# A long convolution fused with an MLP on one core: one chunk of batch 1's first stage ahead of the MLP instead of a chunk and a half

## The chip, the cores and the metric

The kernel runs on one core of a Trainium2 chip. The metric is the device time of one execution in microseconds. The engines are TensorE (PE), VectorE (DVE), ScalarE (ACT), GpSimd (POOL) and SyncE (SP, which here only issues DMAs).

## The reference

```python
def _attn_ref(x, v, pos_emb, w1, w2):            # x, v: (2, 12480, 128)
    h_mlp = np.maximum(pos_emb @ w1, 0.0) @ w2
    h_filt = h_mlp * np.exp(-0.01 * pos)[:, None]
    u = x * v
    y = irfft(rfft(u, 2 * S) * rfft(h_filt, 2 * S))[:, :S]    # along the sequence
    return x * y
def _moe_ref(x, w_in, w_out):                    # x: (24960, 128), w_in: (128, 2048)
    h = x @ w_in
    return np.maximum(0.01 * h, h) @ w_out
```

The output of the first function, both batches behind each other, is the input of the second. All is float32.

## The kernel before, in words

The convolution is a transform in two stages of matmuls each way, over a grid of 98 x 128 points. Per batch there are: stage 1 (98-point transforms of u = x * v, in chunks of 4 columns, 16 chunks), stage 2 (128-point transforms, the product with the filter's spectrum, and the transform back, in 25 chunks of 4 rows), and the last transform, tile by tile (32 tiles of 390 tokens per batch), whose result is multiplied by x, turned, and fed to the MLP. The numbers between the stages go through DRAM (`scr1`, `scr1b`, `scr2`).

Batch 0's stage 1 and 2 run first, alone. Then the MLP's loop over token blocks k and 128-wide parts f of the hidden layer starts (`m1`, `m2`; one pair (k, f) is a step i = 16 k + f of three plus three matmuls). Between its steps, the loop does batch 1's stages 1 and 2 in small pieces: the generator `conv1` (lines 418 to 463), which a `next(conv)` moves on by a piece. Half a chunk of stage 1 is four `next`: at the second of them come 8 matmuls (line 438) and a copy by ScalarE (line 98), then an addition and a subtraction by VectorE (lines 100, 102). "A piece" in this document is such a half chunk. `pace(i)` (line 1207) says how many `next` must be done by step i: none more before step 14, and all of stage 1 by step 120. `AHEAD` is how many were done before the loop.

A chunk of batch 1's stage 1 needs three things first: `fetch_a(c)` (line 240: seven DMAs on SyncE's queue, ft from the table cf, line 243, and x and v, lines 67 and 69), `mult_a(c)` (line 254: GpSimd's product x * v, line 256), and the place of its result `o1`, whose store to `scr1b` (line 460) comes a chunk later. In the steady state of `conv1`, the fetch of chunk c + 1 is issued as chunk c begins, and its product is issued behind chunk c's first half; both hold only from chunk `PRE` on. The chunks below it are fetched and multiplied by other code: chunks 0 and 1 in the loop of batch 0's stage 2 (lines 817 to 820) and behind it (line 863), and chunk `PRE` itself by the MLP's step 2 (`fetch_a(PRE)`, line 1158) and step 9 (`mult_a(PRE)`, lines 1151 and 1160).

Batch 0's stage 2 (lines 807 to 866) works a chunk i as follows: the filter's part (`hp`, line 830, copied by ScalarE, stored as hspec by DMAs of ScalarE's queue, line 840), the forward transform `up` (line 129), six products on VectorE (GpSimd takes one of them, but not in the last two chunks; lines 137 and 138), the transform back of the chunk before (`dp`, line 157), its copies (lines 232 and 795) and stores. Between them, `weights()` (lines 701 to 755) turns the MLP's weights from float64 into pairs of float32 parts. Behind the last chunk stands the handover: the last rows go straight from SBUF into tile 0's input (`last_c`, line 650), tile 1's and 2's inputs are loaded (`upper_c`, `load_gx`, `rows_c`), two pieces of `conv1` are made while tile 0's rows are on their way (lines 1188 to 1194, their VectorE part being put off to lines 1199 and 1155), and tile 0 is transformed (`front0`).

The tiles' inputs pass GpSimd as well (`join_hi`, `join_lo`, lines 668, 677, 680), and so does the second part of the MLP's input (zl, line 950). Each engine works its instructions in the order in which the code issues them.

Of the kernel before, what the change touches and what calls it, by code (L numbers as in the profile page):

```python
# [30 lines left out]
def tile_conv_mlp(ctx, tc, x, v, pos_emb, w1, w2, w_in, w_out, cf, cr, cg, cb, ci, cw, out):  # L31
# [6 lines left out]
    NCH = (NA + KC - 1) // KC  # L38
# [82 lines left out]
    def chunk(c):  # L121
        k0 = c * KC
        return k0, min(KC, NA - k0)
# [112 lines left out]
    with tc.manual_schedule():  # L236
# [3 lines left out]
        def fetch_a(c):  # L240
            ft = s0.tile([128, MC1 * 4 * NA], F32, tag="s0", name="ft1", bufs=3)[:NA].rearrange(
                "a (m p e) -> a m p e", m=MC1, p=2)
            nc.sync.dma_start(out=ft, in_=cf[:, c * MC1:(c + 1) * MC1])
            xv = []
            for i, src in enumerate((x, v)):
                t = s0.tile([128, 1024], F32, tag=f"s{1 + i}", name="xv1", bufs=3 - i)[:NA, :2 * MC1 * D].rearrange(
                    "a (p m d) -> a p m d", p=2, d=D)
                load_tokens(t, src[1], c * MC1, MC1)
                xv.append(t)
            got[c] = ft, xv  # L250
# [3 lines left out]
        def mult_a(c):  # L254
            ft, (xt, vt) = got.pop(c)
            nc.gpsimd.tensor_tensor(out=xt, in0=xt, in1=vt, op=ALU.mult)
            u1[c] = ft, xt
# [155 lines left out]
        psc = {}  # L413
        N1 = HB // MC1
        WAIT = 12
        PRE = 2

        def conv1():
            late = None
            for c in range(N1):  # L420
                if PRE <= c < N1 - 1 and c + 1 not in got:
                    fetch_a(c + 1)
# [7 lines left out]
                for h in range(MC1 // 2):  # L430
# [22 lines left out]
                    yield  # L453
                    if h == 0 and PRE <= c < N1 - 1:
                        mult_a(c + 1)
# [109 lines left out]
        conv = conv1()  # L565
        pieces = N1 * (MC1 // 2) * 4 + WAIT + 3 + 15 * NCH - 3
        A0 = 0
        AHEAD = 1 + 4 * (A0 + 3)

        mlp = ctx.enter_context(tc.tile_pool(name="mlp", bufs=2, reuse_waits="tile"))  # L570
        class Ring:
# [118 lines left out]
        with ExitStack() as st:  # L690
# [66 lines left out]
            load_b(ORD[0])  # L757
            load_b(ORD[1])
            wprep = weights()
            FETCH = [NCH - 5, NCH - 2]  # L760
            late = []
            turn = [0]

# [8 lines left out]
            def ahead(n):  # L772
                for _ in range(4 * n):
                    next(conv)
# [32 lines left out]
            for i, c in enumerate(ORD):  # L807
                if i + 2 < NCH:
                    load_b(ORD[i + 2])
                if NCH - 10 <= i < NCH - 5:  # L810
                    next(first_c)
                if i == NCH - 2:
                    load_gx(0)
                if i == NCH - 1:
                    load_gx(1)
                    rows_c(0, 0, 0, (MID - 2) * KC)
                if i in FETCH:
                    fetch_a(FETCH.index(i))
                if i == NCH - 2:
                    mult_a(0)  # L820
                for f in late:
                    f()
                late = []
                n = chunk(c)[1]
                t, es = bins.pop(c), eh.pop(c)
                hp = two("h")
                for ri in range(2):
                    for k in range(n):
                        h, j = 64 * (k % 2), ri * n // 2 + k // 2
                        nc.tensor.matmul(hp[k % 2][:, D * j:D * j + D], es[h:h + 64, k // 2, ri, :], w22[h:h + 64, :],  # L830
                                         start=True, stop=True)
                hs = sbb.tile([128, 2, KC // 2, 2, D], F32, tag="hs", name="hs", bufs=2)
                for k in range(2):
                    nc.scalar.copy(hs[:, :, :n // 2, k, :],
                                   hp[k][:, :n * D].rearrange("p (r j d) -> p r j d", r=2, d=D))
                hs = hs.rearrange("p r j i d -> p r (j i d)")
                up = two("u")
                fwd(up, lambda s: t[:, :n, s, FO:], n)
                for s in range(2):
                    nc.scalar.dma_start(out=hspec[c][:, :, s, :n * D], in_=hs[HB * s:HB * s + HB, :, :n * D])  # L840
                if i + 1 < NCH:
                    hidden(ORD[i + 1])
                for _ in range(3):
                    next(wprep, None)
                pins[c] = sbb.tile([128, 2, 512], F32, tag="pin", name="pin", bufs=2)
                ab = [sbb.tile([128, 2, 512], F32, tag=g, name=g) for g in ("ta", "tb")]
                product(ab, up, hs, n * D, pins[c], nc.vector if i >= NCH - 2 else nc.gpsimd)
                if i >= 1:
                    b4 = ORD[i - 1]
                    dps[b4] = two("d")  # L850
                    back_halves(dps[b4], pins.pop(b4), b4)
                    evac(b4)
                for _ in range(2):
                    next(wprep, None)
# [3 lines left out]
                    f()  # L858
                late.clear()

            ahead(1)
            run(wprep)
            mult_a(1)
            dps[ORD[-1]] = two("d")
            back_halves(dps[ORD[-1]], pins.pop(ORD[-1]), ORD[-1])
            evac(ORD[-1])
# [283 lines left out]
        at(2, "piece", 0)  # L1150
        at(9, "mult", PRE)

        def do(what, t, i):
            if what == "piece":
                run(pieces_out.pop(0))
                for f in psc.pop("held"):
                    f()
                fetch_a(PRE)
            elif what == "mult":
# [24 lines left out]
        SLOTS = ends[NT] - 14  # L1184
        done = AHEAD
        pieces_out = []
# [27 lines left out]
        for k in range(NTL):  # L1214
            for f in range(NF):
                i = k * NF + f
# [84 lines left out]
```

## Time and profile before

| | |
|---|---|
| median of the runs shown | 1609.13 us |
| lowest run | 1602.2 us |
| the profiled execution's own time | 1607.94 us |
| its span, from the first to the last instruction | 1606.1 us |
| TensorE busy | 1552.2 us, 97% of the span |
| VectorE, ScalarE, GpSimd busy | 71%, 62%, 48% |
| mean granted TensorE clock | 0.985 |

The profile is of one execution. "Busy" leaves out instructions that only issue a DMA or wait. "PEld" is TensorE's loading of weights, beside the matmuls; a float32 matmul of this code counts as two records. The chain of waits goes back from the last instruction to whatever released each one, so a stretch of it that lists only TensorE was bound by TensorE. In a timeline, the square bracket gives how long the engine was idle before the instruction and what released it. "SPq" and "ACTq" are the DMA-issuing instructions of SyncE and ScalarE, and their time is that of the issue, not of the transfer.

### The profile page before, as it was taken

How to read it: one execution, taken by the hardware profiler on the slowest of the kernel's cores; microseconds unless marked ns; L12 is line 12 of the kernel's file. 1: busy time of each engine (PE TensorE's matmuls, PEld its weight loads, DVE VectorE, ACT ScalarE, POOL GpSimd, SP SyncE). 2: the span in 40 equal slices, each digit the busy share in tenths (PEclk: the TensorE clock that was granted, in tenths of full speed). 3: DMA queues.
4: the chain of work that ended last, by engine and by line, in shares of the span. 5: the costliest groups of instructions: out<-in, count | busy, mean ns of one | idle time of the engine just before them, and what ended most of it. 6: DMA issues, size and time to landing. Idle time of an engine off the chain costs nothing.

```text
span 1606.1 us, 27353 instructions
## 1 busy us (share of the span) xinstructions
PE 1552.2 (97%) x9173; PEld 1318.8 (82%) x9173; DVE 1137.9 (71%) x1785; ACT 997.1 (62%) x2108; POOL 766.7 (48%) x806
## 2 busy tenths in 40 slices
PE   7995999899999999999999999999999999999998
PEld 7884555588888888888888888988888888888888
DVE  6884888656985565666676775677777777777776
ACT  2331544446655476777776766667777676777776
POOL 6772212145754275867777774543443433334310
PEclk9997999999999999999999999999999999999999
DMA  9997999866767466756656661421212212121200
GB/s 273 305 314 250 318 317 335 256 196 189 227 199 220 132 190 185 206 158 182 173 167 180 172 163 37 130 86 58 73 54 64 79 58 90 52 64 61 64 11 21
DMA packets 166268, 253.30 MB, mean 158 GB/s; under 512 B 14240, under 2 KB 118932, under 8 KB 163056
## 3 DMA queue, kind: packets, MB, share of 16 engines
q1 hardware_dynamic: 146388, 226.28, 47.4%
q10 hardware_dynamic: 19740, 25.28, 4.6%
q8 instruction: 73, 1.20, 0.3%
q14 instruction: 67, 0.55, 0.1%
HBM read 168.03 MB, written 83.43 MB: 157 GB/s over the span
## 4 chain that ended last, share of the span: by engine, by line
PE 75%; DMA 12%; DVE 7%; ACT 2%; issue 2%; SPq 1%; POOL 0%; ACTq 0%; DVEq 0%; POOLq 0%
PE mh L993 28%; PE acc L1035 9%; PE acc L1034 9%; PE acc L1036 9%; PE yp L917 4%; PE cv L143 3%; DMA scr<-o 3%; PE cv L438 3%; DMA scr<-ct 3%; PE op L1066 2%; PE a L392 2%; PE up L129 2%; PE zp L936 1%; DMA ft<-in_cf_dram 1%; PE dp L157 1%
## 5 line engine op out<-in xcount | busy, mean ns | idle before, releaser
L998 DVE SCALAR_TENSOR_TENSOR rl<-mh,rh 128x512 fp32r<-128x512 f32 (+1 forms) x336 | 226.9, 682 | 203.2 <-ACT rh L997 201.8
L1006 DVE TENSOR_TENSOR rl<-mh,rh 128x512 fp32r<-128x512 f32 (+2 forms) x416 | 277.1, 670 | 83.7 <-ACT rh L1005 75.1
L1001 ACT ACTIVATE mh<-mh 128x512 f32<-128x512 f32 (+2 forms) x416 | 236.4, 569 | 154.1 <-PE mh L993 141.1
L993 PE MATMUL mh<-zh,w_in_h 128*128 128x512 f32 (+3 forms) x800 | 316.8, 396 | 3.4 <-DVE rl L998 2.3
L993 PE MATMUL mh<-zl,w_in_h 128*128 128x512 f32 (+3 forms) x800 | 300.1, 375 | 0.0
L993 PE MATMUL mh<-zh,w_in_l 128*128 128x512 f32 (+3 forms) x800 | 299.9, 375 | 0.0
L1035 PE MATMUL acc<-rl,w_out_h 128*128 128x512 f32 (+3 forms) x800 | 299.3, 374 | 0.1
L1034 PE MATMUL acc<-rh,w_out_h 128*128 128x512 f32 (+3 forms) x800 | 299.3, 374 | 0.0
L1036 PE MATMUL acc<-rh,w_out_l 128*128 128x512 f32 (+3 forms) x800 | 299.0, 374 | 0.0
L997 ACT ACTIVATE rh<-mh 128x512 fp32r<-128x512 f32 (+1 forms) x336 | 198.9, 595 | 138.8 <-PE mh L993 130.1
L950 POOL TENSOR_TENSOR zl<-zf,zh 128x390 fp32r<-128x390 f32 (+24 forms) x110 | 68.4, 634 | 402.4 <-ACT zh L949 386.1
L680 POOL TENSOR_TENSOR cp<-cq,cp 98x256 f32<-98x256 f32 x248 | 193.3, 780 | 31.4 <-DVE cp L668 14.7
L1003 DVE CAST rh<-mh 128x512 fp32r<-128x512 f32 (+2 forms) x208 | 139.3, 670 | 65.9 <-ACT mh L1001 65.6
L993 PEld LDWEIGHTS mh<-zh,w_in_h 128*128 128x128 f32 x800 | 151.9, 190 | 29.4 <-DVE rl L998 8.4
L993 PEld LDWEIGHTS mh<-zh,w_in_l 128*128 128x128 f32 x800 | 151.9, 190 | 19.8
L1035 PEld LDWEIGHTS acc<-rl,w_out_h 128*128 128x128 f32 x800 | 151.3, 189 | 20.3 <-DVE rl L1006 0.4
L1034 PEld LDWEIGHTS acc<-rh,w_out_h 128*128 128x128 f32 x800 | 151.3, 189 | 19.8
L1036 PEld LDWEIGHTS acc<-rh,w_out_l 128*128 128x128 f32 x800 | 151.3, 189 | 19.8
L993 PEld LDWEIGHTS mh<-zl,w_in_h 128*128 128x128 f32 x800 | 152.3, 190 | 15.2 <-DVE zl L982 0.2
L1005 ACT CAST rh<-mh 128x512 fp32r<-128x512 f32 (+2 forms) x208 | 118.5, 570 | 6.5
L677 POOL TENSOR_TENSOR cq<-cin 98x256 f32<-98x256 f32 x124 | 97.1, 783 | 0.5 <-DMA cin<-scr 0.4
L138 POOL TENSOR_TENSOR pin<-ta,tb 128x512 f32<-128x512 f32 (+1 forms) x23 | 28.8, 1252 | 134.9 <-DVE tb L137 134.9
(166 smaller groups left out, 2545.7 us busy)
## 6 DMA issues: line engine op xcount, KB each, us to landing
cin<-scr SPq DMA_DIRECT2D x318, 98.0 KB
hd<-hspec SPq DMA_DIRECT2D x48, 512.0 KB
bin<-scr SPq DMA_DIRECT2D x24, 768.0 KB
scr<-o SPq DMA_DIRECT2D x28, 588.0 KB
scr<-ct SPq DMA_DIRECT2D x25, 512.0 KB
scr1b<-o SPq DMA_DIRECT2D x32, 392.0 KB
hspec<-hs ACTq DMA_DIRECT2D x48, 256.0 KB
xm<-in_x_dram SPq DMA_DIRECT2D x128, 96.0 KB
```

Source lines behind the costliest of these rows:

```text
L677: eng.tensor_tensor(out=cq[:, p], in0=ci_t[:, 0, :, 0, :], in1=ci_t[:, 0, :, 1, :], op=op)
L680: eng.tensor_tensor(out=cp[:, p, w], in0=cq[:, p], in1=cp[:, p, 1], op=op)
L993: nc.tensor.matmul(hp, u[:, fs], m, start=(i == 0), stop=(i == 2))
L997: nc.scalar.activation(out=split2(rh), in_=plain(hp), func=AF.Relu)
L998: nc.vector.scalar_tensor_tensor(out=split2(rl), in0=plain(hp), scalar=0.0, in1=split2(rh), op0=ALU.max, op1=ALU.subtract)
L1001: nc.scalar.activation(out=hp, in_=hp, func=AF.Lrelu, alpha=0.01)
L1003: nc.vector.tensor_copy(split2(rh), plain(hp))
L1005: nc.scalar.copy(split2(rh), plain(hp))
L1006: nc.vector.tensor_tensor(out=split2(rl), in0=plain(hp), in1=split2(rh), op=ALU.subtract)
L1034: nc.tensor.matmul(ap, w_out_h[:, f, :], rh, start=(f == 0 and not sums(k)), stop=False)
L1035: nc.tensor.matmul(ap, w_out_h[:, f, :], rl, start=False, stop=False)
L1036: nc.tensor.matmul(ap, w_out_l[:, f, :], rh, start=False, stop=(f == NF - 1))
```

## The change

Of chunks 0 and 1, only chunk 0 is fetched and multiplied in batch 0's stage 2, and no piece is made there: the call `ahead(1)`, `mult_a(1)` and the second fetch go. `PRE` is 1 instead of 2, so chunk 1 is the one that step 2 fetches and step 9 multiplies, and `conv1` fetches chunk 2 itself, as it begins chunk 1. `AHEAD` is 9 instead of 13, so that `pace` spreads four `next` more over the steps 14 to 120.

```diff
-        PRE = 2
+        PRE = 1
...
-        AHEAD = 1 + 4 * (A0 + 3)
+        AHEAD = 1 + 4 * (A0 + 2)
...
-            FETCH = [NCH - 5, NCH - 2]
...
-                if i in FETCH:
-                    fetch_a(FETCH.index(i))
+                if i == NCH - 5:
+                    fetch_a(0)
                 if i == NCH - 2:
                     mult_a(0)
...
-            ahead(1)
             run(wprep)
-            mult_a(1)
             dps[ORD[-1]] = two("d")
```

Chunk 1 begins, in `conv1`, at the end of the second piece of the handover, where the loads of tile 2 have not been issued yet. So chunk 2 is fetched there, ahead of chunk 1. On SyncE's queue the handover reads as follows in the kernel before, from the last load of tile 1 (`cin`, line 643) over tile 2's loads to the store of chunk 0 and the fetch of chunk 2:

```order
L643 DMA cin<-scr_0_63 49x512 x2
L622 DMA cin<-scr_0_63 49x512 x3
L626 DMA cin<-scr_0_63 49x2x128 x2
L643 DMA cin<-scr_0_63 49x512 x2
L602 DMA gt<-in_cg_dram 49x392 x2
L608 DMA xm<-in_x_dram 48x2x256 x2
L610 DMA xm<-in_x_dram 1x2x256
L613 DMA xm<-in_x_dram 1x256
L460 DMA scr1b<-o_1265 98x4x256 x2
L243 DMA ft_3126<-in_cf_dram 98x1568
```

and in the changed kernel, from the same load of tile 1 on:

```order
L643 DMA cin<-scr_0_63 49x512 x2
L243 DMA ft_3017<-in_cf_dram 98x1568
L67 DMA xv_3019<-in_x_dram 96x2x512
L67 DMA xv_3019<-in_x_dram 1x2x512
L69 DMA xv_3019<-in_x_dram 1x2x512
L67 DMA xv_3023<-in_v_dram 96x2x512
L67 DMA xv_3023<-in_v_dram 1x2x512
L69 DMA xv_3023<-in_v_dram 1x2x512
L622 DMA cin<-scr_0_63 49x512 x3
L626 DMA cin<-scr_0_63 49x2x128 x2
L643 DMA cin<-scr_0_63 49x512 x2
L602 DMA gt<-in_cg_dram 49x392 x2
```

A whole fetch, chunk 2's, has come in between tile 1's and tile 2's loads; the fetch of chunk 1 follows where that of chunk 2 stood, behind the store of line 460.

On TensorE, the end of batch 0's stage 2 and the handover up to tile 0's transform (`yp`, `zp`) read, in the kernel before (the number in a name tells the tiles of chunk 0, xv_2618, from those of chunk 1, xv_2834):

```order
L129 MATMUL up<-bin,mb 64x512 x4
L746 MATMUL wcp<-wo,wts 128x128 x2
L157 MATMUL dp<-pin,mi_69 128x512 x4
L438 MATMUL hp<-xv_2618,ft_2616 98x128 x8
L157 MATMUL dp<-pin,mi_69 128x512 x4
L438 MATMUL cv<-xv_2618,ft_2616 98x128 x8
L438 MATMUL cv<-xv_2834,ft_2832 98x128 x8
L965 MATMUL yp<-cp,gt 64x128 x8
```

and in the changed kernel, whose lines behind the change are three lower (L962 is L965 before):

```order
L129 MATMUL up<-bin,mb 64x512 x4
L746 MATMUL wcp<-wo,wts 128x128 x2
L157 MATMUL dp<-pin,mi_69 128x512 x8
L438 MATMUL cv<-xv_2618,ft_2616 98x128 x16
L962 MATMUL yp<-cp,gt 64x128 x8
```

The piece between the two groups of L157 is gone, and the two pieces of the handover are both chunk 0's.

## Rows read from the trace of the kernel before

**Rows 1.** The page's first line.

```profile
span 1606.1 us, 27353 instructions
```

**Rows 2.** Windows: stretch, length, busy us (records) by engine, PEclk, DMA share, GB/s.

```profile
340.00:360.00 20.00, 20.00 (x134) 18.64 (x133) 9.57 (x17) 10.79 (x25) 10.78 (x14) 1.00 0.62 177
...
420.00:440.00 20.00, 19.78 (x140) 17.46 (x139) 18.76 (x22) 11.39 (x23) 15.56 (x13) 1.00 0.71 220
...
480.00:600.00 120.00, 119.31 (x721) 105.36 (x720) 73.13 (x115) 67.45 (x138) 53.33 (x57) 1.00 0.63 180
```

**Rows 3.** Chain of waits, 290 to 320 us: start, length, what.

```profile
291.65 4.71 DMA gt<-in_cg_dram
...
296.39 0.52 ACTq L840
...
308.43 0.64 PE wcp L746 x4
...
310.99 1.92 PE hp L438 x16
312.91 3.01 PE dp L157 x8
...
315.94 0.70 DVE ct L795
```

**Rows 4.** Timeline of the same end of stage 2, all engines.

```profile
284.68 0.43 DVE L740 TENSOR_TENSOR w_out_l<-wo,w_out_h 128x256 fp32r<-128x256 f32 x1 [3.31 <-ACT w_out_h L738]
...
297.58 1.16 PE L830 MATMUL hp<-w,es 64*128 64x128 f32 x16 [2.18 <-ACT es L786]
...
307.18 2.36 POOL L256 TENSOR_TENSOR xv<-xv,xv 98x1024 f32<-98x1024 f32 x1 [7.46 <-DMA xv<-in_v_dram]
...
307.83 1.99 DVE L740 TENSOR_TENSOR w_out_l<-wo,w_out_h 128x256 fp32r<-128x256 f32 x1 [1.08 <-ACT w_out_h L738]
...
313.17 0.69 DVE L138 TENSOR_TENSOR pin<-ta,tb 128x512 f32<-128x512 f32 x1
...
313.92 0.30 PEld L157 LDWEIGHTS dp<-pin,mi 64*128 64x128 f32 x4 [0.79 <-DVE pin L138]
```

**Rows 5.** Timeline, TensorE, the handover's pieces and tile 0's transform.

```profile
315.84 3.74 PE L438 MATMUL cv<-xv,ft 98*98 98x128 f32 x32
...
320.92 1.07 PE L965 MATMUL yp<-cp,gt 98*64 98x128 f32 x8 [1.34 <-issue]
```

**Rows 6.** Chain of waits: one piece in the loop.

```profile
347.95 1.75 PE cv L438 x16
```

**Rows 7.** Timeline, SyncE's DMA issues of a store and of two fetches.

```profile
329.81 0.84 SPq L460 DMA_DIRECT2D scr1b<-o  x2
...
335.85 0.57 SPq L69 DMA_DIRECT2D xv<-in_v_dram  x1
...
352.83 0.33 SPq L243 DMA_DIRECT2D ft<-in_cf_dram  x1
...
356.46 0.57 SPq L69 DMA_DIRECT2D xv<-in_v_dram  x1
```

**Rows 8.** Timeline, GpSimd, products of two chunks and what follows.

```profile
342.55 2.36 POOL L256 TENSOR_TENSOR xv<-xv,xv 98x1024 f32<-98x1024 f32 x1
346.91 0.41 POOL L950 TENSOR_TENSOR zl<-zf,zh 128x122 fp32r<-128x122 f32 x1 [2.00 <-ACT zh L949]
...
360.97 2.37 POOL L256 TENSOR_TENSOR xv<-xv,xv 98x1024 f32<-98x1024 f32 x1 [7.44 <-DMA xv<-in_v_dram]
```

**Rows 9.** Windows behind the handover's pieces.

```profile
320.00:322.00 2.00, 1.06 (x8) 0.61 (x8) 1.90 (x5) 0.20 (x1) 0.00 (x0) 1.00 0.71 196
322.00:324.00 2.00, 1.08 (x9) 0.75 (x10) 0.83 (x3) 0.00 (x0) 0.00 (x0) 0.76 0.46 169
```

**Rows 10.** Waits of GpSimd, 340 to 560 us: total, times, longest.

```profile
POOL xv L256 <- DMA xv<-in_v_dram: 36.3, 7, 11.5
```

**Rows 11.** Group of the pieces' matmuls, 326 to 600 us: busy, mean, idle before.

```profile
L438 PE MATMUL cv<-xv,ft 98*98 98x128 f32 x464 | 56.3, 273 | 0.7 <-DVE o L102 0.7
```

## The prediction

> **What bounds the kernel now.** I read the page's head first: one execution spans 1606.1 us [rows 1] and was timed at 1607.94 us, so 1.84 us lie around the span. Then the busy time by stretch: from 340 us on TensorE is busy 20.00 of 20 us, and still 119.31 of 120 us from 480 to 600 us [rows 2]. So in the MLP every matmul added costs its own time, and work on other engines costs nothing until one of them fills up: VectorE has 18.76 of 20 us between 420 and 440 us, while TensorE still has 19.78 [rows 2].
>
> The place of the change is the handover from batch 0's second stage to the MLP, 290 to 350 us. There I read the chain of waits [rows 3]. From 297.58 us [rows 4] to 315.92 us the chain is TensorE alone, and the piece of batch 1's convolution that the change takes away stands in it with 1.92 us (L438 at 310.99), directly ahead of the last chunk's inverse matmuls (L157, 3.01 us). Behind them come the copy on VectorE at 315.94, three small DMA issues, and the DMA that hands the last rows to tile 0. A chain only says what came last, so I asked the timeline what the L157 matmuls would have waited for without the piece [rows 4]. Their weight load at 313.92 waited 0.79 us for VectorE's product (L138, 313.17 to 313.86). So VectorE, not the piece, sets the end of this stage; the piece sat in TensorE's gap.
>
> VectorE itself was held there. L740 took 1.99 us where the same instruction took 0.43 us at 284.68, and it ended at 309.82, 0.28 us behind GpSimd's product of chunk 1 (L256, 307.18 to 309.54) [rows 4]. GpSimd started that late because it waited 7.46 us for chunk 1's v rows. The change removes that product from this place.
>
> **The change, part by part.** The instruction totals of the built program do not change on any engine; all terms are moves.
>
> (a) Stage end, removed: chunk 1's fetch (seven DMAs; by the shapes 98 x 1568 floats of cf and twice 98 x 1024 of x and v, 1.42 MB), GpSimd's product, and a first piece (8 matmuls, one ScalarE copy, two VectorE operations). Without the GpSimd product L740 ends at 307.83 + 0.43 = 308.26. The next VectorE instruction then waits for the wcp matmul, which ends at 308.43 + 0.64 = 309.07 [rows 3]. So the VectorE series that ran without a gap from 309.82 to 313.86 starts at about 309.1: **0.7 us earlier**. TensorE follows it, since the piece is gone. Bounds: 0 if another wait holds VectorE; 1.92 us, the chain's price of the piece, if TensorE's order alone had mattered. I take 0.7, the nearest rows. The piece's ScalarE copy and VectorE operations came after the product, in idle time, and are worth nothing. The freed DMA bandwidth is worth nothing on a chain that is TensorE from 297.58 on.
>
> (b) The handover keeps two pieces (now chunk 0's halves instead of chunk 0's second and chunk 1's first): 3.74 us from 315.84, in the wait for tile 0's rows. The first transform starts at 320.92 after an idle time of 1.34 us [rows 5], so they stay covered, in either version.
>
> (c) The MLP gets one piece more: 1.75 us of TensorE by the chain at 347.95 [rows 6], **+1.75 us**. TensorE has no idle time to take it. Its VectorE part, two operations on 512 columns like L138 with its 0.69 us [rows 4], is hidden wherever VectorE is not full; by the stretch 420 to 440 it might not be, which would add up to 1.4 us. From below: 0, if the piece falls where TensorE waits anyway. I take 1.75.
>
> (d) Moved on SyncE: chunk 2's fetch (seven issues) now stands ahead of tile 2's loads, and chunk 1's fetch takes chunk 2's old place behind the store of chunk 0. A fetch issued without hindrance takes 352.83 to 357.03, 4.2 us [rows 7]. So tile 2's loads start that much later, and so does the fetch behind them. Its last issue, at 335.85, becomes 340.05. The chunk that was fetched at 352.83 had its last issue at 356.46, and GpSimd, waiting for it, began at 360.97 [rows 7, 8]: 4.5 us from issue to use. So chunk 1 is there at 344.55; GpSimd, which in the old order took its chunk at 342.55 without a wait [rows 8], multiplies 344.6 to 346.9. The first piece in the MLP stood at 347.95 and would stand 0.7 us earlier at most: no stall, with a margin of 0.3 to 1 us. Two microseconds of GpSimd's waiting are covered by the 2.00 us it idled behind the old product [rows 8]. Cost 0; from above see the second rival.
>
> Sum: 1607.94 - 0.7 + 1.75 = **1609.0 us**. The median shown is 1609.13, the lowest run 1602.2; the profiled execution lies 1.2 us under that median, so the sum stands at the median too. It is no change that could be told: about 2% (32 us) is what a measurement of this kernel can tell.
>
> **Weighed against a page.** In the two stretches from 320 to 324 us TensorE was busy 1.06 and 1.08 of 2 us, and its granted clock, 1.00 in the first, was 0.76 on the mean of the second: it fell there from its upper level, 2.4 GHz, to its lower, 1.2 GHz [rows 9]. What the engine did before the fall was to work in two short bursts, waiting for VectorE between them; (a) leaves a like gap ahead of L157's last matmuls, where the piece stood. The Trainium skill ("TensorE: Matmul & The Clock Gate", Part 1, "What's actually happening") has the clock follow how busy the engine was shortly before, which speaks against this change. If the new gap lowers the clock, the third rival's time follows; the sum leaves it out, because the gap is one where those two stretches had several.
>
> **Rivals.**
>
> *The stage end gains more.* ScalarE's issue of hspec at 296.39 had to wait for the landing of gt (291.65 + 4.71), and TensorE idled 2.18 us behind it [rows 3, 4]. Chunk 1's cf was issued just there. If its absence lets hspec go up to 1 us earlier, TensorE starts 1 us earlier, and with (a) the end moves 1.7 us; if TensorE also keeps its upper clock behind the shorter gap, I estimate as much again. Against: tile 1's gt and x loads move up into the same place. Time 1609.0 - 1.0 to - 2.0, say 1607.5.
>
> *The late chunk, slower.* Place: the first in-loop piece, behind GpSimd's product of chunk 1. If the two fetches are issued hindered, as at 329.81 to 336.42 where store and fetch took 6.6 us, of which the store 0.8 [rows 7], each takes 5.8 instead of 4.2 us. It decides from a last issue later than 347.25 - 2.36 - 4.5 = 340.4 us; each microsecond beyond is one of TensorE. The shift of one fetch and tile 2's loads behind it being also slowed gives 1.5 to 3 us: 1610.5 to 1612, say 1611.5. For it: the margin is under 1 us. Against: SyncE idles later and the older fetch had 2 us to spare.
>
> *The clock falls at the stage end, slower by a little.* Last inverse matmuls and the two pieces at the low level: the pieces take up to 3.7 us more, 1.3 of it covered, the matmuls 1 us, up to 3.4 us; part returns if the stretch behind 323 us then runs at the upper level. Time 1609 to 1612, say 1610.5.
>
> *GpSimd's waits reach TensorE.* GpSimd waited 36.3 us in seven products for v rows between 340 and 560 us, and none of it reached TensorE, whose waits behind VectorE for the pieces are 0.7 us in all [rows 10, 11]. All pieces now stand at other steps. If that cover were lost wholly: 1609.0 + 36 = 1645, over 2% slower. For it only that the cover is a matter of order; against: the steps of fetch, product and use keep their distance to each other from chunk 2 on.
>
> **How the numbers follow.** Forecast 0.5 (1609.0); stage end gains more 0.17; late chunk 0.18; clock 0.12; GpSimd's waits 0.03. The forecast's own bounds are -1.2 (all of the 1.92 gained) and +2.1 (nothing gained, VectorE full), 1607.8 to 1611.1; the first three rivals stretch this from 1607 to 1612.4. The runs of the kernel before differ by 7 us themselves, so I reach to 1601 and 1616. The last rival lies outside. Faster by over 2% has no mechanism: 0.01. Slower by over 2% is the last rival's, of its 0.03: 0.02. Within 2%: 0.97.
>
> **What would show it.** Right: L740 near 0.43 us; the copy L795 on VectorE about 0.7 us earlier; no L438 in the chain ahead of L157; the loop's 29 pieces (464 records, 16 a piece [rows 11]) become 30 at the same price; GpSimd's product of chunk 1 begins at 344 to 345 us, with 1 to 2 us of wait for v; TensorE idle for about 0.7 us from 480 to 600 us, as before. Wrong: TensorE waiting at the first in-loop L438; a granted clock under 1 from 313 to 318 us; a first MLP matmul more than 2 us from its old place; idle time of TensorE in later stretches.

## The result, and the profile after

The changed kernel takes 1617.2 us (median), the kernel before 1606.5 us beside it. Executions in the chip's slow state, such as one of the kernel before at 3284 us, are left out of all medians, differences and ratios here. The ratio is 1.007, with a 95% interval of 1.0056 to 1.0084. That is no change at the 2% that the prediction counted with, but 10.7 us of loss where the prediction's sum had 1.05 us, and a time outside its range of 1601 to 1616 us.

The page's first line of the changed kernel, which answers to [rows 1]; lines of the code behind the change are three lower than before:

```profile
span 1614.9 us, 27364 instructions
```

Its span is 8.8 us longer. The end of stage 2 and the handover come first, in the timeline (start, length, engine, line, what it does, and in brackets the idle time ahead and who ended it), which answers to [rows 4] and [rows 5]:

```profile
310.77 0.43 DVE L740 TENSOR_TENSOR w_out_l<-wo,w_out_h 128x256 fp32r<-128x256 f32 x1 [1.85 <-ACT w_out_h L738]
...
311.34 0.71 PE L746 MATMUL wcp<-wo,wts 128*128 128x128 f32 x4
...
316.28 0.30 PEld L157 LDWEIGHTS dp<-pin,mi 64*128 64x128 f32 x4 [1.35 <-DVE pin L138]
...
318.20 3.73 PE L438 MATMUL cv<-xv,ft 98*98 98x128 f32 x32
318.31 0.69 DVE L794 COPY ct<-dp 128x512 f32<-128x512 f32 x1 [1.88 <-PE dp L157]
...
323.18 1.07 PE L962 MATMUL yp<-cp,gt 98*64 98x128 f32 x8 [1.25 <-issue]
```

L740 takes 0.43 us, as forecast, and no L438 stands ahead of the last L157, which waits for VectorE's product as [rows 4] suggested. The two handover pieces take 3.73 us, and the transform behind them is still ready late (1.25 us idle): they are covered. So this place is as predicted.

The windows of [rows 2], now:

```profile
340.00:360.00 20.00, 17.59 (x107) 16.26 (x106) 7.77 (x14) 8.81 (x24) 14.49 (x17) 0.91 0.69 200
420.00:440.00 20.00, 18.87 (x108) 16.51 (x108) 15.26 (x19) 12.80 (x24) 18.47 (x16) 1.00 0.59 176
480.00:600.00 120.00, 120.00 (x742) 106.62 (x741) 74.01 (x116) 65.10 (x134) 51.53 (x56) 1.00 0.61 177
```

From 340 to 360 us TensorE has lost 2.4 of 20 us, and its clock 9%. From 420 to 440 us it has lost 1.1. From 480 to 600 us TensorE waits for nothing. So most of the loss lies in the first part of the MLP's loop. The chain of waits (start, length, what) says what came there:

```profile
327.88 6.99 DMA xv<-in_v_dram
334.88 4.01 DMA cin<-scr
...
344.69 5.25 DMA xv<-in_v_dram
...
350.24 2.35 POOL xv L256
352.64 3.53 PE cv L438 x16
```

Read it upwards from the piece (352.64): it waited for GpSimd's product of chunk 1, this for the v rows of chunk 1, whose last issue was at 344.69. The loads of tile 2 in front of that (334.88) waited for the rows of chunk 2. Of the rows left out, 3.9 us are GpSimd's sums for a tile (339.49 to 343.36). This is the late chunk, the prediction's second rival. SyncE's issues show how the queue got there; [rows 7] has the same before:

```profile
325.48 0.32 SPq L243 DMA_DIRECT2D ft<-in_cf_dram  x1
...
329.19 0.57 SPq L69 DMA_DIRECT2D xv<-in_v_dram  x1
329.87 4.07 SPq L622 DMA_DIRECT2D cin<-scr  x3
...
340.05 0.58 SPq L243 DMA_DIRECT2D ft<-in_cf_dram  x1
...
344.69 0.57 SPq L69 DMA_DIRECT2D xv<-in_v_dram  x1
```

The fetch put ahead costs 4.28 us (325.48 to 329.76), as forecast. What was not forecast is the next row: the first load of tile 2 takes 4.07 us to issue behind it. What SyncE's queue waited for there (total, times, longest) says why: 3.1 us for the fetch's own rows to land.

```profile
SPq L622 <- DMA ft<-in_cf_dram: 2.1, 1, 2.1
SPq L622 <- DMA xv<-in_x_dram: 1.0, 1, 1.0
```

The last issue is at 344.69, where the prediction had 340.05.

Granted clock (the number behind the five engines' busy times) at three places:

```profile
313.00:318.00 5.00, 3.81 (x14) 1.11 (x10) 3.36 (x6) 1.93 (x4) 0.00 (x0) 1.00 0.81 241
326.00:330.00 4.00, 3.30 (x10) 2.42 (x11) 2.48 (x7) 1.11 (x4) 1.46 (x2) 0.50 0.92 237
352.90:356.30 3.40, 3.40 (x17) 3.40 (x16) 0.00 (x0) 0.10 (x1) 3.40 (x6) 0.50 0.51 151
```

At the end of the stage the clock stays at 1.00, the upper level. Behind the piece's wait it is 0.50 for 3.4 us, so that the piece of [rows 6], 1.75 us there, takes 3.53 us.

Last, the group of the pieces' matmuls, which answers to [rows 11]:

```profile
L438 PE MATMUL cv<-xv,ft 98*98 98x128 f32 x480 | 60.0, 278 | 5.8 <-DVE o L102 3.6 <-POOL xv L256 2.2
```

480 records instead of 464, the one piece more; and 5.8 us of idle time ahead of them instead of 0.7, of which 3.6 us for VectorE's subtraction (L102) that frees the piece's second bank (one of the two buffers that its matmuls write). Where one of the three such waits comes from can be read at 400 us:

```profile
400.47 2.37 POOL L256 TENSOR_TENSOR xv<-xv,xv 98x1024 f32<-98x1024 f32 x1
...
401.17 2.23 DVE L1016 TENSOR_TENSOR rl<-r,rh 128x512 fp32r<-128x512 f32 x1 [2.81 <-ACT rh L1015]
...
403.32 1.04 PE L438 MATMUL cv<-xv,ft 98*98 98x128 f32 x8
403.32 0.68 DVE L100 TENSOR_TENSOR o<-cv,a1s 98x512 f32<-98x512 f32 x1
...
404.97 0.68 DVE L102 TENSOR_TENSOR o<-cv,a1s 98x512 f32<-98x512 f32 x1
...
405.71 1.12 PE L438 MATMUL cv<-xv,ft 98*98 98x128 f32 x8 [1.36 <-DVE o L102]
```

GpSimd's product of a chunk (L256) runs from 400.47 to 402.84 us. VectorE's L1016, which takes 0.67 to 1.22 us where it starts outside such a product, starts inside it, after VectorE had been idle for 2.81 us, and takes 2.23 us; the addition (L100) and the subtraction (L102) of the piece before come behind it; and TensorE, in the middle of its next piece, waits 1.36 us for them. The other two waits, at 428 and 471 us, have the same three links: an L256 at 422.80 and 464.15 us, an L1016 of 2.77 us and a pair of 4.00 us that start in it, then L100 and L102. The Trainium skill ("SBUF — State Buffer", "SBUF: two separate sides") has GpSimd and a VectorE operation with two SBUF inputs exclude each other for a whole instruction; L1016 has two such inputs (r and rh), and its end 0.56 us behind L256's agrees.

Such a meeting alone costs TensorE little. The kernel before has them too (there the line is L1019), with as long a hold (under the product from 420.59 us on), and its next piece waits 0.22 us; and in the changed kernel a fourth one, at 475.30 us, is followed by no wait of a piece over 0.2 us:

```profile
420.08 3.88 DVE L1019 TENSOR_TENSOR rl<-r,rh 128x512 fp32r<-128x512 f32 x2
```

```profile
475.30 1.99 DVE L1016 TENSOR_TENSOR rl<-r,rh 128x512 fp32r<-128x512 f32 x1 [0.19 <-ACT rh L1015]
```

What differs is how soon behind the hold the next piece needs the bank. That is a reading of the rows; no run moves a GpSimd product alone.

### The profile page after: what moved, and what is told of

Same layout as the page of the kernel before. It is cut to its first block, busy times and chain, and to the rows that moved or that the text cites. A ratio compares the mean times of both kernels' runs of the same rounds, so it can differ in the third digit from the quotient of the medians.

```text
span 1614.9 us, 27364 instructions
## 1 busy us (share of the span) xinstructions
PE 1552.5 (96%) x9173; PEld 1318.8 (82%) x9173; DVE 1131.0 (70%) x1785; ACT 995.5 (62%) x2108; POOL 762.9 (47%) x806
## 4 chain that ended last, share of the span: by engine, by line
PE 76%; DMA 11%; DVE 6%; ACT 3%; issue 2%; SPq 2%; POOL 1%; ACTq 0%; DVEq 0%; POOLq 0%
PE mh L990 28%; PE acc L1032 9%; PE acc L1033 9%; PE acc L1031 9%; PE yp L914 4%; PE cv L438 3%; PE cv L143 3%; DMA scr<-ct 3%; DMA scr<-o 3%; PE op L1063 2%; PE up L129 2%; PE a L392 1%; PE zp L933 1%; DMA ft<-in_cf_dram 1%; PE dp L157 1%
## 5 line engine op out<-in xcount | busy, mean ns | idle before, releaser
L680 POOL TENSOR_TENSOR cp<-cq,cp 98x256 f32<-98x256 f32 x248 | 193.4, 780 | 24.8 <-DVE cp L668 8.0
L668 POOL TENSOR_TENSOR cp<-cin 98x256 f32<-98x256 f32 x78 | 56.6, 744 | 76.3 <-DMA cin<-scr 29.9
```

What stands on the lines that cost most here:

```text
L680: eng.tensor_tensor(out=cp[:, p, w], in0=cq[:, p], in1=cp[:, p, 1], op=op)
```

## The experiments

Two theories stood after this. *Late chunk and steps*: the loss is the piece (1.75 us), the late chunk (3.7 us), and the waits for VectorE that come because every piece now stands at another step (3 us). *A price of the piece*: a piece moved from the handover into the loop costs all of it, wherever it stands. All ratios are to the kernel before, which ran beside. A wait is placed by the step that begins behind it, one more than the i of `pace`; a piece by the i at which its matmuls are issued.

**1. The fetch order repaired.** The changed kernel, with chunk 1 fetched where chunk 2 was:

```diff
-                    fetch_a(c + 1)
+                    fetch_a(PRE if c == PRE else c + 1)
...
-                fetch_a(PRE)
+                fetch_a(PRE + 1)
```

> The changed kernel, but the handover fetches chunk 1 ahead of tile 2's loads and step 2 fetches chunk 2 (the other way round before). Theory A (chunk 1 came late because its fetch stood behind chunk 2's and tile 2's loads): GpSimd's product of chunk 1 starts at most 19 us after the first MLP matmul instead of 22.4, the first piece in the loop waits for nothing and takes 1.75 us at the full clock instead of 2.15 us of waiting and 3.2 us at the lower level; 3.7 us come back, ratio to the kernel before about 1.0035 to 1.005 instead of 1.007. Rival (the order of the two fetches does not matter, the moved piece and its new steps cost it all): ratio 1.0065 to 1.0075, the wait at the first piece stays or moves elsewhere.

1611.72 us, ratio 1.0036 (1.0021 to 1.0052). GpSimd's product comes without a wait, and so does the piece; the waits for VectorE remain:

```profile
341.77 2.37 POOL L256 TENSOR_TENSOR xv<-xv,xv 98x1024 f32<-98x1024 f32 x1
```

```profile
L438 PE MATMUL cv<-xv,ft 98*98 98x128 f32 x480 | 58.4, 274 | 3.1 <-DVE o L102 3.1
```

About 4 to 5 of the 10.7 us were the late chunk's.

**2. The piece alone.** The kernel before with one piece fewer ahead, and its fetches and products left alone:

```diff
-        AHEAD = 1 + 4 * (A0 + 3)
+        AHEAD = 1 + 4 * (A0 + 2)
...
-            ahead(1)
```

> The kernel before with one part of the change alone: chunks 0 and 1 are both fetched and multiplied in stage 2 as before, but no piece is made there, so the loop does one piece more at the changed kernel's steps. Theory A: no late chunk; cost is the piece (1.75 us) and the longer waits of pieces for VectorE (2.9 us), less nothing at the stage end, since GpSimd's product still holds VectorE there: about 4.5 us, ratio 1.002 to 1.004. Rival (the piece and its steps are the whole loss): ratio 1.006 to 1.0075.

1611.52 us, 1.0036 (1.0021 to 1.005), the same as run 1. So where chunk 1 is fetched and multiplied, if it is in time, makes no difference that can be told, and the rest of the loss is the piece with what it brings along:

```profile
L438 PE MATMUL cv<-xv,ft 98*98 98x128 f32 x480 | 58.3, 274 | 4.0 <-DVE o L102 4.0
```

**3. The fetch put off.** The changed kernel, but chunk 2 is fetched only as the loop begins chunk 1:

```diff
-                if PRE <= c < N1 - 1 and c + 1 not in got:
+                if PRE < c < N1 - 1 and c + 1 not in got:
...
+                        if c == PRE:
+                            fetch_a(c + 1)
```

> The changed kernel, but chunk 2 is fetched only when the loop begins chunk 1 (step 14 or 15), so nothing stands ahead of tile 2's loads and chunk 1's fetch goes out at step 2 as chunk 2's did in the kernel before. Theory A: GpSimd's product of chunk 1 starts 16 to 18 us after the first MLP matmul, no wait and no fall of the clock at the first piece in the loop, ratio 1.0035 to 1.005. Then chunk 2 could be late instead, some 5 steps on: a wait of up to 4 us for it at its first piece would put the ratio back to 1.006. Rival: 1.0065 to 1.0075 without a wait for a product anywhere.

1618.55 us, 1.0077 (1.0058 to 1.0096): a miss. Chunk 1's two pieces no longer wait, but chunk 2 is late in its place, by more, at its first piece (line 440 here is line 438 before):

```profile
366.14 3.73 PE L440 MATMUL cv<-xv,ft 98*98 98x128 f32 x16 [4.56 <-DMA ft<-in_cf_dram]
```

The row names the table's DMA, but the piece's weights were loaded at the same moment, 0.05 us behind the end of GpSimd's product of chunk 2 (363.75 to 366.09 us), which itself had waited for the v rows. This is no repair, but it shows the same thing at another chunk: a fetch issued only a few steps ahead of its piece ends up on TensorE.

**4. A slower pace.** Run 1, with the pieces up to step 120 as far apart as before and the missing four `next` at step 120:

```diff
-                return AHEAD + (STAGE1 - AHEAD) * max(0, i - FROM) // (TILL - FROM)
+                return AHEAD + (STAGE1 - AHEAD - 4) * max(0, i - FROM) // (TILL - FROM)
```

> As the first of these kernels, but the loop's pieces stand at the steps at which the kernel before had its pieces (115 moves of the generator over the steps 14 to 119), and the four moves left over are all made at step 120. Theory B (the other part of the loss is that pieces 4% closer together run into VectorE's fullest stretch, where each piece must wait for the subtraction of the one before it): waits of pieces for VectorE fall from 3.6 to under 1.5 us, ratio lower than the first kernel's by 0.001 to 0.002. Rival (these waits come from chance, not from the steps): same ratio as the first kernel within 0.0007, waits of 2 us or more.

1615.0 us, 1.0051 (1.0032 to 1.0071): a miss. Of the waits for VectorE 1.0 us is left in the stretch and 1.1 us comes at step 121, where two pieces are close; and a transform now waits for GpSimd's sums instead (L914 for L680, 1.9 us in two waits). The pieces do stand at the very steps of before here (15, 19, 23, 26, 30, 34 and so on). But with one piece more, each of them is the other half of its chunk. A chunk's first half, behind which GpSimd's product of the next chunk is issued, stood at steps 19, 26, 34, 41 before and stands at 23, 30, 38, 45 now, so GpSimd's products and the fetches fall elsewhere. The steps of the pieces alone aren't it.

**5 and 6. More ahead, and denser without the change.** Run 5 is the kernel before with three pieces in the handover instead of two, and with chunk 2 fetched there and chunk 3 at step 2; run 6 the kernel before with nothing but a steeper pace, so that its pieces stand closer:

```diff
-                    fetch_a(c + 1)
+                    fetch_a(PRE if c == PRE else c + 1)
...
-        AHEAD = 1 + 4 * (A0 + 3)
+        AHEAD = 1 + 4 * (A0 + 4)
...
-                fetch_a(PRE)
+                fetch_a(PRE + 1)
...
+        psc["next"] = lambda: [ps.tile([128, WIDE], F32, tag="mh", name="cv", bufs=3) for _ in range(2)]
+        for _ in range(4):
+            next(conv)
...
```

> The other direction: the kernel before with one piece more ahead of the loop, so two whole chunks. Chunk 0's second half goes to two of the mh banks and is finished on VectorE ahead of tile 0's rows, chunk 1's halves follow; the handover has three pieces, the loop 28 instead of 29, and chunk 2 is fetched in the handover, chunk 3 at step 2. Theory A (a piece costs the loop 1.75 us, and closer pieces wait for VectorE): the loop is 1.75 to 2.5 us shorter than the kernel before's, tile 0's transform is up to 0.5 us later as the third piece ends behind the rows' arrival, unless TensorE keeps its upper clock through the handover, which would give 2 us more; ratio 0.9975 to 0.9995. Rival (the handover has no more room: three pieces delay the first MLP matmul by their length): ratio 1.000 to 1.001.

```diff
-                return AHEAD + (STAGE1 - AHEAD) * max(0, i - FROM) // (TILL - FROM)
+                return min(STAGE1, AHEAD + (STAGE1 - AHEAD + 4) * max(0, i - FROM) // (TILL - FROM))
```

> The kernel before, with nothing moved, but the loop's pieces at the changed kernel's spacing (119 moves of the generator over 106 steps from step 14 on, so that stage 1 ends at step 117). Theory B (the spacing alone makes the pieces wait for VectorE): pieces at the steps 41, 52 and 73 wait 2.9 to 4 us in all for the subtraction before them, where it was 0.7; ratio 1.001 to 1.0025. Rival (these waits belong to the piece that was moved in, or to the other fetch order): 0.7 us of waits, ratio 0.9995 to 1.0005.

Run 5: 1610.66 us, 1.0032 (1.0015 to 1.005), although the loop has a piece less. The pieces wait 2.8 us for VectorE, and here too a GpSimd product falls into the wrong place, between two of the sums that a transform needs:

```profile
404.70 2.53 POOL L256 TENSOR_TENSOR xv<-xv,xv 98x1024 f32<-98x1024 f32 x1
...
407.19 1.18 POOL L680 TENSOR_TENSOR cp<-cq,cp 98x256 f32<-98x256 f32 x1
...
408.42 1.12 PE L917 MATMUL yp<-cp,gt 98*64 98x128 f32 x6 [2.08 <-POOL cp L680]
```

Run 6: 1608.11 us, 1.002 (1.0008 to 1.0033), with the work of the kernel before and its order up to the loop. Its profiled execution (1613.48 us) was the slowest of its twelve, but shows what the steps alone can do, in the waits (total, times, longest) and in the clock behind the longest of them:

```profile
PE cv L438 <- DVE o L102: 3.3, 2, 2.4
```

```profile
464.50:471.30 6.80, 6.58 (x20) 5.59 (x21) 2.48 (x5) 1.83 (x4) 0.15 (x1) 0.50 0.45 112
```

Its pieces stand at the changed kernel's steps but are the other halves, and its two waits come at steps 70 and 73: the changed kernel's waits at steps 41 and 52, which were expected here too, are gone. So, as in run 4, the waits hang on how the pieces stand to the work that moves with the halves.

**7. The changed kernel again**, unedited.

> The changed kernel once more, unedited, for a second trace of it and more times. If its loss lies in the loop alone, the loop takes 6.8 us more than in the kernel before also in this trace, and the ratio falls towards 1.0045 with more runs; if the ratio stays at 1.006 to 1.0075 with the same loop, 3 to 4 us are lost ahead of the loop or the late chunk's wait differs between executions.

1615.88 us, 1.0053 (1.0037 to 1.007). The late chunk is there again; the piece waits 2.41 us:

```profile
348.47 2.35 POOL L256 TENSOR_TENSOR xv<-xv,xv 98x1024 f32<-98x1024 f32 x1 [5.38 <-DMA cin<-scr]
...
350.87 1.99 PE L438 MATMUL cv<-xv,ft 98*98 98x128 f32 x16 [2.41 <-POOL xv L256]
```

```profile
352.00:356.00 4.00, 4.00 (x26) 3.76 (x25) 1.82 (x4) 1.94 (x4) 4.00 (x4) 1.00 0.47 157
469.50:472.90 3.40, 3.40 (x10) 2.69 (x9) 1.91 (x2) 1.04 (x3) 2.35 (x1) 0.50 0.92 267
```

This time the clock stays up behind it. It fell later, at 469.5 us, behind a wait of 1.56 us for VectorE. So the waits belong to the program; which of them the clock answers belongs to the execution.

**8. The steps of before.** Run 5's three pieces ahead, but then every piece, as the same half of the same chunk, at exactly the step of the kernel before, whose first one is gone (and chunks 2 and 3 fetched at steps 2 and 18):

```diff
-                return AHEAD + (STAGE1 - AHEAD) * max(0, i - FROM) // (TILL - FROM)
+                return max(AHEAD, AHEAD - 4 + (STAGE1 - AHEAD + 4) * max(0, i - FROM) // (TILL - FROM))
```

> The kernel before with one convolution piece more made ahead in the handover (three pieces there), and then the pieces left at exactly the steps at which the kernel before makes them, only without its first one (step 16); chunk 2 is fetched at step 2 and chunk 3 at step 18, as before. From step 20 on the loop is the one before. Theory (what a piece in the loop costs is its own 1.7 us and the waits that its step brings, so what the other versions lost they lost by the steps): the loop is 1.7 us shorter than before's, the pieces wait for VectorE's subtraction some 0.7 us in all as before, near steps 57, 72 and 75, GpSimd's sums hold no product of TensorE near step 45; ratio 0.9985 to 0.9995. Rival (a piece more in the handover costs there what it saves in the loop, or the waits fall elsewhere although the steps are the same): 1.000 or more.

1604.45 us, 0.9996 (0.9982 to 1.001). The interval holds both theories' ratios, but against run 5 it is 0.0036 lower, with the same work in the loop at other steps and two fetches moved, and the waits are the old ones:

```profile
L438 PE MATMUL cv<-xv,ft 98*98 98x128 f32 x448 | 54.4, 273 | 0.8 <-DVE o L102 0.8
```

**9. The changed kernel with both repairs**: run 1, with the pieces at the steps of before, and the extra one at step 14.

```diff
-                return AHEAD + (STAGE1 - AHEAD) * max(0, i - FROM) // (TILL - FROM)
+                if i < FROM:
+                    return AHEAD
+                return AHEAD + 4 + (STAGE1 - AHEAD - 4) * (i - FROM) // (TILL - FROM)
```

> The changed kernel with two repairs: chunk 1 is fetched in the handover and chunk 2 after it (as in e1_swap), and the pieces in the loop stand at exactly the steps of the kernel before, with the one that the change adds ahead of them, at step 14. So it has the change's extra piece, but neither its late chunk nor its denser steps. Theory (the loss is the piece, the late chunk and the waits that the new steps bring): the loop is 1.6 to 1.8 us longer than before's up to step 160, the pieces wait for VectorE's subtraction 0.7 to 0.8 us in all, near steps 57, 72 and 75, no low clock between steps 16 and 160; the wait at step 167 goes one way or the other by up to 2.8 us; ratio 0.9995 to 1.0015, against 1.0036 of e1_swap. Rival (a piece more in the loop brings its waits wherever it stands): the loop 3 us longer or more at step 160, the waits over 2 us, ratio as e1_swap's, 1.003 or more.

1612.01 us, 1.0031 (1.0016 to 1.0046): the rival's ratio. The waits for VectorE are the theory's, but another has come:

```profile
PE yp L914 <- POOL cp L680: 1.2, 2, 0.8
...
PE cv L438 <- DVE o L102: 0.8, 3, 0.3
```

The transform of tile 2 waits 1.2 us at step 11 for GpSimd's sums, whose rows (cin) came late: a whole fetch still stands ahead of tile 2's loads on SyncE. The changed kernel has 0.3 us of this, so its fetch order has a second price that varies with the execution. The loop is 3.7 us longer at step 160, where the theory had 1.6 to 1.8: the piece takes 2.1 of it (steps 14 to 16), and the rest is this wait and small ones. In the medians the run loses 5.8 us, and some 2 to 3 us of that are not explained.

**10 and 11. The kernel before again**, two profiles.

> The kernel before, unedited, for a second profile of it: how much of what its first profile shows belongs to the kernel and how much to that execution. Theory (what comes of the order of the instructions repeats, what comes of the clock and of DMA does not): the waits for VectorE's subtraction again 0.7 to 0.8 us at steps 57, 72 and 75, none at the first in-loop piece; the first MLP matmul anywhere from 323.5 to 328 us. Open: whether the wait of some 2 us at step 167 is again followed by 3.4 us at half clock. If it is not, the 2.8 us that the changed kernel got back there were a fall of the clock in the one profile of before, and no gain of the change. Rival (the profile repeats, the fall at step 167 with it): the loop within 0.5 us of the first profile's 1280.3 us.

> The same once more, a third profile of the kernel before, with the same two theories: by the first the loop is 2.3 to 3.4 us shorter than in the first profile if the clock stays up at step 167, by the second it is within 0.5 us of it.

1603.6 and 1603.5 us, one execution each. The waits for VectorE are 0.4 us in both, at steps 57 and 75, and the loop is 2.0 and 2.6 us shorter than in the first profile. TensorE's waits of run 10, and the clock behind the first of them, which ends at 632.7 us (step 167):

```profile
PE cv L143 <- ACT ct L223: 1.2, 1, 1.2
...
PE cv L438 <- DVE o L102: 0.4, 2, 0.2
```

```profile
633.00:636.40 3.40, 3.25 (x15) 2.53 (x14) 1.90 (x4) 3.40 (x8) 1.21 (x1) 1.00 0.21 58
```

The profile on which the prediction rests had this wait at 1.96 us, until 636.3 us, and behind it:

```profile
637.10:640.50 3.40, 3.40 (x10) 2.63 (x9) 2.41 (x5) 3.29 (x8) 1.72 (x2) 0.50 0.21 59
```

No other profile has a fall at this step, not even run 2's, whose wait there was 2.2 us. Against that first profile the changed kernel seems to get back 2.8 us between steps 160 and 176 (its wait is 0.4 us); against these two it is 0.6 us. Most of that gain was the one profile's. The base for the loop is the mean of these two, 1278.0 us. Both were quick executions, 2 to 3 us under the kernel's medians of about 1606 us, so the differences from this base may be high by as much.

**12. Only the piece, at the steps of before.** Run 2, with run 9's pace: the fetches, the products and SyncE's order are those of before, each piece is the same half as before at the same step, and the extra piece stands at step 14.

> The kernel before with one piece fewer made ahead and nothing else moved: fetches, products and SyncE's order as before, and in the loop the pieces at the steps of before, with the extra one ahead of them at step 14. So of the change only the piece is left, without its fetch order and its denser steps. Theory: the loop is 1.6 to 2.1 us longer up to step 160 than in the profiles of before, the pieces wait for VectorE 0.4 to 0.8 us in all as there, GpSimd's sums hold nothing at step 11 (in e9_steps they held 1.2 us, with tile 2's rows behind a whole fetch); ratio 1.000 to 1.002. Rival (a piece more in the loop costs 5 us wherever it stands): ratio 1.003 or more, and the profile shows where.

1608.8 us, 1.0015 (1.0003 to 1.0027), 2.9 us over the kernel before. Nothing waits that did not wait before:

```profile
PE cv L143 <- ACT ct L223: 1.5, 1, 1.5
...
PE cv L438 <- DVE o L102: 0.4, 2, 0.2
```

Runs 2 and 12 differ in the pace alone, and so in the steps of the pieces and of the products behind them: 0.0021 of ratio, 3.4 us, for the same work (the two intervals just overlap). The three runs that keep the halves of before at the steps of before (8, 9, 12) wait 0.4 to 0.8 us for VectorE, all other changed ones 2.1 us or more.

All profiles side by side; the loop is the span less the start of the first MLP matmul, and the last column the difference of the medians of the kernel and of the kernel before that ran beside it, without the executions left out above:

| profile | span | loop | loop, less 1278.0 | waits for L102 | medians |
|---|---|---|---|---|---|
| before, shown ahead | 1606.1 | 1280.3 | +2.3 | 0.7 | |
| before, 10 and 11 | 1601.7, 1601.7 | 1278.3, 1277.7 | | 0.4, 0.4 | |
| changed, and run 7 | 1614.9, 1614.1 | 1287.1, 1287.7 | +9.1, +9.7 | 3.6, 4.3 | +10.7, +9.6 |
| 1 | 1608.0 | 1283.4 | +5.4 | 3.1 | +5.6 |
| 2 | 1608.5 | 1284.7 | +6.7 | 4.0 | +5.4 |
| 3 | 1615.3 | 1290.3 | +12.3 | 3.3 | +12.4 |
| 4 | 1614.7 | 1286.8 | +8.8 | 2.1 | +8.8 |
| 5 | 1610.5 | 1284.7 | +6.7 | 2.8 | +4.4 |
| 6 | 1611.6 | 1284.8 | +6.8 | 3.3 | +1.9 |
| 8 | 1603.3 | 1276.8 | -1.2 | 0.8 | -0.8 |
| 9 | 1610.0 | 1282.0 | +4.0 | 0.8 | +5.8 |
| 12 | 1607.0 | 1280.7 | +2.7 | 0.4 | +2.9 |

But for runs 5 and 6, whose profiled executions were 2.0 and 5.4 us slower than their medians, the loop's difference is the median's to 1.8 us. So what the change costs, it costs mainly in the loop. The first MLP matmul starts at 323.4 to 326.8 us in the kernels with the stage 2 of before or with its fetches and products, and at 324.6 to 328.0 us in those with the changed one. The two overlap, so no gain or loss of a microsecond ahead of the loop can be told.

## Why the prediction was wrong

**(a) Stage end, -0.7 us: right in its mechanism, but no gain against two of the three profiles of the kernel before.** L740 fell from 1.99 to 0.43 us, and from the end of the `wcp` matmuls to VectorE's copy it is 6.26 us (312.05 to 318.31) instead of the 6.87 us of [rows 3] (309.07 to 315.94): 0.6 of the 0.7 us. That VectorE and not the piece sets this end is right too. But run 10, the kernel before with its piece, has 6.25 us as well:

```profile
307.12 0.71 PE L746 MATMUL wcp<-wo,wts 128*128 128x128 f32 x4
...
314.08 0.69 DVE L795 COPY ct<-dp 128x512 f32<-128x512 f32 x1 [0.41 <-PE dp L157]
```

With GpSimd's product in stage 2, L740 took 0.42 us in runs 10 and 11, 0.43 to 0.75 us in runs 12, 2 and 6, and 2.13 and 2.16 us in runs 5 and 8. The 1.99 us of [rows 4] was a meeting of two instructions that some executions have, not a fixed price. And the first MLP matmul moves by 2.5 us between the three profiles of the kernel before (323.4 to 325.8 us), so a term of 0.7 us there could not be told in the time.

**(b) The handover's pieces: right**, 3.73 us and covered.

**(c) The piece in the loop, +1.75 us: the price of the piece is right, and the step is mis-sized.** Run 12 has the piece at a harmless place: +2.7 us in the loop (2.1 of it by step 160), +2.9 us in the medians, of which the chain's 1.75 us is the larger part. But with one piece more in the loop every piece becomes the other half of its chunk, so that all products and fetches move, and from the sixth on (step 33 instead of 34) the pieces' steps as well. (c) priced one piece. The prediction put the waits for VectorE at "up to 1.4 us", as a matter of VectorE being full. They rose by 3.2 us (3.6 against the 0.4 of runs 10 and 11), and not because VectorE was full: from 420 to 440 us it was busy 18.76 of 20 us before [rows 2] and 15.26 after (at somewhat earlier steps), and the waits grew. In the changed kernel's trace they came where a GpSimd product held VectorE's operation directly ahead of L100 and L102 and the next piece was close. That the moved steps bring them is shown by run 12 against run 2; the hold is read from the rows.

**(d) The fetch order, cost 0: this step failed.** Its working took the fetch put ahead at 4.2 us, which held (4.28), and added nothing for the loads behind it. The load of tile 2 behind the fetch took 4.07 us to issue, 3.1 us of it waiting for the fetch's rows to land, and this execution's first MLP matmul was 2.0 us later. The trace of before had both prices of this load, at 323.05 us without a fetch ahead of it and at 336.53 us behind one:

```profile
323.05 0.99 SPq L622 DMA_DIRECT2D cin<-scr  x3
...
336.53 4.05 SPq L622 DMA_DIRECT2D cin<-scr  x3
```

With the difference of 3.1 us the working gives 340.05 + 3.1 + 2.0 = 345.2, and the last issue came at 344.69. From issue to use it was 5.55 us (344.69 to 350.24) instead of 4.5. The rival *late chunk* named the place, the mechanism and the point from which it decides, and gave 1611.5 us; its price was 1.5 to 3 us, and the wait was 2.15 us, so it was right so far. It left out that the clock may fall behind such a wait, which it did here and not in run 7; that stretched the piece (3.53 us, against 1.99 in run 7 at the upper clock) and brought the price to 3.7 us.

**The sum.** In the changed kernel's loop: late chunk 3.7, piece 1.75, waits for VectorE 3.2, tile 2's sums 0.3; together 8.95 us, less the 0.6 us got back at step 167, where the loop is 9.1 us longer than the base. Run 1 without the first is at +5.4, run 12 without the first and third at +2.7. Run 9, which lacks the same two, is at +4.0 and +5.8 in the medians, so the sum isn't closed there. Of the 10.7 us between the medians 1.6 us are not in the loop's difference; in run 7 the two agree (9.6 and 9.7).

**The other rivals.** *The stage end gains more* didn't show. *The clock falls at the stage end*: it was 1.00 from 313 to 318 us, and 0.50 from 326 to 330, where it fell before as well [rows 9]. *GpSimd's waits reach TensorE* had a true core, that the work beside TensorE now falls at other steps (the first five pieces in fact keep theirs), but looked at the waits for v rows, and the link ran through VectorE.

**The range** was too narrow above because the rivals were priced one at a time: late chunk and full VectorE together gave 1612.9 with the prediction's own numbers, and the clock's share (1.5) with the waits beyond 1.4 us (1.8) brings it to 1616.2. The last microsecond, to 1617.2, is not assigned. And the sum's base, 1607.94 us, was itself 1.4 us above the 1606.5 us at which the kernel before ran beside the changed one.

## What to carry to other kernels

When a change shifts a table of steps, price all the entries that move, not only the one that is added: run 12 against run 2 is the same work at other steps, and 3.4 us. Keeping the steps is not enough if other work then stands at them, as in run 4: try the added item with the others, half for half, where they were. Look for pairs whose meeting can reach the engine that bounds (here a GpSimd product and VectorE's operation ahead of the one that frees a bank), and at how soon the bank is needed. When a transfer is put ahead of others in one queue, add to its own issue time what the next load loses behind it, and profile the kernel before more than once before a term of a few tenths, or a gain "given back", is believed.

## What was not expected of the hardware

A wait of TensorE of some 2 us inside the busy loop can be followed by 3.4 us, in run 6 by 6.8 us, at a granted clock of 0.50: after 2.15 us in the changed kernel, 1.56 us in run 7, 1.96 us in the first profile of before, 2.44 us in run 6. Runs 4 and 5 have 3.4 us of it too, from 410.41 and 408.24 us on, at their waits for GpSimd's sums (1.22 and 0.70 us, and 2.08 us), and run 3 has 6.8 us from 365.00 us on, in its wait of 4.56 us. But it need not follow: after 2.41 us in run 7 and 2.18 us in run 2 the clock stayed at 1.00. The Trainium skill ("TensorE: Matmul & The Clock Gate", Part 1, "What's actually happening") has the clock follow how busy the engine was shortly before; the falls agree with it, and so may the one that did not come, but no row here tells which wait will be followed by one. As a price, the wait may count nearly twice: in the changed kernel 2.15 us of waiting and 1.5 us of a slower piece.
